# A decode step of adaLN, grouped-query attention and a token MLP: wider matmuls, another order of the rounds, and 96 rows of the output weights in transfers of 8 rows

## The chip, the cores and the metric

The kernel runs on one core of one Trainium2 chip. The metric is the time of one execution in microseconds (us) on the device; the number to compare is the median over several executions. Three executions of the kernel before took 396.08, 396.34 and 397.13 us.

## What is computed

All arithmetic is float32. There are four sequences (B = 4), each with one new token of width D = 512, 32 query heads in 8 groups of 4 (HKV = 8, REP = 4), and caches of 4096 keys and values of width 128 for each group. F = 1792.

```python
mod = silu(c) @ w_mod                 # (4, 512) @ (512, 6*512): sa, ca, ga, sb, cb, gb
h = layernorm(x) * (1 + ca) + sa
q = h @ wq                            # 4 x 32 heads of 128
o = softmax(q @ k^T / sqrt(128)) @ v  # k, v: (4, 8, 4096, 128), 4 queries share one k, v
x = x + ga * (o @ wo)
h = layernorm(x) * (1 + cb) + sb
u = gelu(layernorm(h)[:, :, None] * w1 + b1)   # (4, 512, 1792)
x = x + gb * (u @ w2 + b2)
```

Two caches of 67 MB each are read once; with the weights the kernel reads 157.32 MB.

## The kernel before, in words

One pair of a sequence b and a key head h is called head i, with i = 8 b + h from 0 to 31. For each head one tile of keys (2 MB, `load_k`, L168) and one tile of values (2 MB, `load_v`, L173) are loaded. Those tiles, the query weights and the modulation weights share a ring of five buffers (L35), so a load may be issued once the tile five places before it in the ring has been used. All loads are issued from SP, in the order of the program: keys of head i+3, then values of head i+1. Behind the values of heads 0 to 7 follows 1 MB of output weights each (`wo_t`, L181), which stay; behind heads 2, 4 and 31 follow modulation weights. The keys of head 31 come between the values of heads 28 and 29, and the last loads are the values of head 29 and 30 in two pieces each, those of head 31 in four, and 1 MB of modulation weights.

Every instruction stands where the code puts it: no scheduler moves it, and each engine takes its instructions in program order. A head passes these steps:

- `scores(i)` (L200): eight matmuls, 512 keys each, into four groups of 32 output partitions; then VectorE takes the maximum (L208).
- `colmax(i)` (L211) and `expo(i)` (L219): the maximum is brought together over the partitions by a transpose (L214), a small reduction (L216) and a small matmul (L223), and ScalarE takes the exponential (L228).
- `transposes(i)` (L231): eight transposes of the exponentials, one matmul for the sums (L237), and a copy to SBUF (L238).
- `values(i)` (L248): 32 matmuls with 128 columns, one for every 128 of the 4096 values; then a copy `po` (L259).
- `project_a(i)` (L266) folds the four partition groups and divides by the sum (`pt`, copied to `oT` at L271); `project_b(i)` (L274) multiplies by the output weights in 16 matmuls of 128 columns (L282) and adds into `acc` (L290).

Round i of the main loop (L446) does these for several heads: loads, `transposes(i+1)`, `project_a(i-1)`, `scores(i+2)`, `project_b(i-1)`, `colmax(i+2)`, `expo(i+2)`, a piece of the epilogue of the sequence before, `values(i)`. The epilogue (L362) is the second layer norm and the MLP of a sequence whose eight heads are done: `expand` on VectorE (L354), Gelu on ScalarE (L379), `contract` on TensorE (L359). In the profile its pieces stand in the first five rounds of the next sequence. The last sequence is done in `finish` (L391). In round 25 the gate of the residual is folded into the output weights of head 31 (`fold_gate`, L429), so that its projection can be added to the residual in PSUM (`pgx`).

In the profile a float32 matmul is two weight loads and two multiplications; a transpose is one of each.

Of the kernel before, what the change touches and what calls it, by code (L numbers as in the profile page):

```python
# [23 lines left out]
# 1/sqrt(v): integer seed RS0 - bits(v) / 2, read as a negative float, then a  # L24
# quadratic step y = y (v y^2 - RS1) and a cubic one y = y ((v y^2 - RS2) v y^2 + RS3);
# the seed's scale makes the product of the steps' leading factors one.
# [5 lines left out]
def adaln_decode(ctx: ExitStack, tc: tile.TileContext, small, x, wmod, wq, kT, v, wo, out):  # L32
# [39 lines left out]
    grp = cst.tile([P, 4, 32], F32, name="grp")  # L72
    dv.tensor_copy(grp, g32.unsqueeze(1).to_broadcast([P, 4, 32]))
    grp = grp.rearrange("p c r -> p (c r)")
    sel0 = g32[:, 0:REP]
    diag = ident.rearrange("p (c r) -> p c r", c=4)[:, :, 0:1]
# [5 lines left out]
    for i in range(2):  # L82
        t = cst.tile([P, 8, 4, 32], F32, name=f"pT{i}")
        dv.memset(t, 0.0)
        pTs.append(t)
    wo_t = [cst.tile([P, REP, D], F32, name=f"wo{h}") for h in range(HKV)]
    prep = cst.tile([P, 4, B, P], F32, name="prep")
    osb = cst.tile([P, B, P], F32, name="osb")

# [24 lines left out]
    dv.tensor_mul(sT.rearrange("p k b -> p (k b)"), sg, cT)  # L114

# [36 lines left out]
    px = ps_e.tile([P, B, P], F32, name="px", tag="e")  # L152
    for b in range(B):
        for c in range(4):
            mm(px[32 * c:32 * c + 32, b, :], ident[0:B, b:b + 1].to_broadcast([B, 32]),
               xr[:, c * P:(c + 1) * P], start=True, stop=True)
# [15 lines left out]

    def load_v(i):  # L173
# [6 lines left out]
        if i < HKV:  # L180
            nc.sync.dma_start(wo_t[i], wo[i])  # L181
# [5 lines left out]
    def modmm(pm, t, steps):  # L187
        for b, k in steps:
            for c in range(4):
                mm(pm[32 * c:32 * c + 32, b, :], sT[:, k, b:b + 1].to_broadcast([P, 32]),  # L190
                   WM[t][:, k, c * P:(c + 1) * P], start=(k == 0), stop=(k == 3))

    def mod(t):
        pm = ps_e.tile([P, B, P], F32, name=f"pm{t}", tag="e")
        modmm(pm, t, [divmod(e, 4) for e in range(4 * B)])
        return pm
# [14 lines left out]
    def colmax(i):  # L211
        s, m = S[i]
        pm = ps_m.tile([1, P], F32, name="pm", tag="m")
        nc.tensor.transpose(pm, m, ident)  # L214
        mx = wk.tile([1, 32], F32, name="mx")
        dv.tensor_reduce(mx, pm.rearrange("o (c r) -> o r c", c=4), axis=AX.X, op=OP.max)  # L216
        S[i] = [s, mx]

    def expo(i):  # L219
        s, mx = S[i]  # L220
        pb = ps_m.tile([P, 1], F32, name="pb", tag="m")
        for c in range(4):
            mm(pb[32 * c:32 * c + 32, :], mx, neg1, start=True, stop=True)  # L223
# [7 lines left out]
    def transposes(i):  # L231
        s, p, l = S.pop(i)
        pt = s.rearrange("p (k n) -> p k n", k=8)
        for k in range(8):
# [3 lines left out]
        dv.tensor_copy(pTs[i % 2][:, :, :, 0:REP],  # L238
                       pt.rearrange("p k (c r) -> p k c r", c=4)[:, :, :, 0:REP])
        rl = wk.tile([P, 1], F32, name="rl")  # L240
        dv.reciprocal(rl, pl)
        sel = wk.tile([P, REP], F32, name="sel", bufs=3)
        dv.tensor_scalar(sel, sel0, rl, None, op0=OP.mult)
# [4 lines left out]
    def values(i, ks):  # L248
        if ks[0] == 0:
            PV[i] = ps_v.tile([P, DH], F32, name="pv")  # L250
        pv = PV[i]
        for k in ks:
            for c in range(4):
                mm(pv[32 * c:32 * c + 32, :], pTs[i % 2][:, k, c, :], VT[i][:, k * 4 + c, :],  # L254
                   start=(k == 0), stop=(k == 7))
        if ks[-1] < 7:
            return
        po = wk.tile([P, DH], F32, name="po")
        dv.tensor_copy(po, pv)  # L259
        SP[i] = (SEL.pop(i), po)  # L260

    ACC = {}

    OT = {}

    def project_a(i):  # L266
        sel, po = SP.pop(i)
        pt = ps_m.tile([P, REP], F32, name="pt", tag="m")
        mm(pt, po, sel, start=True, stop=True)  # L269
# [4 lines left out]
    def project_b(i, pa=None):  # L274
        b, h = divmod(i, HKV)
        oT = OT.pop(i)
        folded = pa is not None
        if not folded:
            pa = ps_m.tile([P, P], F32, name="pa", tag="m")
        for g in range(REP):  # L280
            for c in range(4):
                mm(pa[32 * c:32 * c + 32, :], oT[:, g:g + 1].to_broadcast([P, 32]),  # L282
                   wo_t[h][:, g, c * P:(c + 1) * P], start=(g == 0 and not folded), stop=(g == REP - 1))
        if folded:
            return
        if h == 0:
            ACC[b] = wk.tile([P, P], F32, name="acc")
            dv.tensor_copy(ACC[b], pa)
        elif h < HKV - 1:
            dv.tensor_add(ACC[b], ACC[b], pa)  # L290
            if h == HKV - 2:
                ap_ = wk.tile([P, P], F32, name="ap")
                dv.tensor_mul(ap_, ACC.pop(b), prep[:, 1, b])
                dv.tensor_add(ap_, ap_, prep[:, 0, b])
                EP[b] = ap_
        else:
            x1 = XK[:, b]
            dv.tensor_mul(x1, pa, prep[:, 1, b])
            dv.tensor_add(x1, x1, EP.pop(b))

    EP = {}
# [3 lines left out]
    def stats(xin):  # L305
# [3 lines left out]
        dv.tensor_mul(sm_, st.unsqueeze(1).to_broadcast([P, 4, 6]), diag.to_broadcast([P, 4, 6]))  # L309
# [13 lines left out]
    def adaln(b, pst):  # L323
# [4 lines left out]
            a, XK[:, b], mean, prep[:, 3, b], op0=OP.subtract, op1=OP.mult))  # L328
        dv.scalar_tensor_tensor(h1, a, r, prep[:, 2, b], op0=OP.mult, op1=OP.add)
        return h1, stats(h1)  # L330

    def bcast(h1, pb=None):
        if pb is None:
            pb = ps_e.tile([P, 4, P], F32, name="phb", tag="e")
        for c in range(4):
            mm(pb[:, c, :], ident[:, 32 * c:32 * c + 1].to_broadcast([P, P]), h1, start=True, stop=True)
# [24 lines left out]

    def epilogue(b):  # L362
        stm = stats(XK[:, b])
# [4 lines left out]
        hb, wr = affine(pst, bcast(h1))  # L368
# [152 lines left out]
```

## Time and profile before

| | |
|---|---|
| median of three executions | 396.34 us (396.08 to 397.13) |
| profiled execution, from the first to the last instruction | 394.4 us |
| TensorE, matmuls | 288.9 us busy, 5414 records |
| TensorE, weight loads | 194.4 us busy, 5414 records |
| VectorE | 151.4 us busy, 487 instructions |
| ScalarE | 96.4 us busy, 119 instructions |
| mean granted TensorE clock | 0.943 |
| read from memory | 157.32 MB, 399 GB/s over the span |

The profile shows one execution. Its own span is 394.4 us; the median of the timed executions lies 1.9 us above it, which is taken as what lies around the span. A row of a timeline gives the start in us, the length in us, the engine, the line, the operation, and in brackets the idle time before it with what ended that. A count behind a row is that of merged instructions. In the rows by stretches (windows) each engine's busy time is followed by the number of its instructions; the last three numbers are the granted TensorE clock, the busy share of the 16 DMA engines, and GB/s.

### The profile page before, as it was taken

How to read it: one execution, taken by the hardware profiler on the slowest of the kernel's cores; microseconds unless marked ns; L12 is line 12 of the kernel's file. 1: busy time of each engine (PE TensorE's matmuls, PEld its weight loads, DVE VectorE, ACT ScalarE, POOL GpSimd, SP SyncE). 2: the span in 40 equal slices, each digit the busy share in tenths (PEclk: the TensorE clock that was granted, in tenths of full speed). 3: DMA queues.
4: the chain of work that ended last, by engine and by line, in shares of the span. 5: the costliest groups of instructions: out<-in, count | busy, mean ns of one | idle time of the engine just before them, and what ended most of it. 6: DMA issues, size and time to landing. Idle time of an engine off the chain costs nothing.

```text
span 394.4 us, 11762 instructions
## 1 busy us (share of the span) xinstructions
PE 288.9 (73%) x5414; PEld 194.4 (49%) x5414; DVE 151.4 (38%) x487; ACT 96.4 (24%) x119; POOL 0.7 (0%) x6
## 2 busy tenths in 40 slices
PE   0976785539967586778677787779776787897884
PEld 0122444408745444556455455557544464675763
DVE  4222222203222232556432334546323345763266
ACT  1001111101110111136641011348411010685125
POOL 0000000000000000000000000000000000000000
PEclk9989689959999889999999899989999898999999
DMA  8999999999999999999999999999999999999700
GB/s 321 425 430 437 431 419 433 420 430 433 429 420 432 429 429 429 427 432 429 429 421 429 430 434 429 424 425 431 432 429 427 425 429 434 427 425 417 289 8 2
DMA packets 12720, 158.08 MB, mean 401 GB/s; under 512 B 1516, under 2 KB 1532, under 8 KB 1920
## 3 DMA queue, kind: packets, MB, share of 16 engines
q1 hardware_dynamic: 12672, 157.34, 93.9%
q8 instruction: 42, 0.69, 0.6%
q14 instruction: 6, 0.05, 0.0%
HBM read 157.32 MB, written 0.01 MB: 399 GB/s over the span
## 4 chain that ended last, share of the span: by engine, by line
DMA 56%; PE 29%; DVE 8%; ACT 4%; issue 1%; SPq 0%; ACTq 0%; DVEq 0%
DMA k<-in_kT 43%; DMA v<-in_v 11%; PE s L205 10%; PE pv L254 5%; DVE m L208 3%; PE s L126 2%; PE s L235 2%; DMA sm<-in_small 2%; PE py L359 2%; DVE u L354 1%; PE pa L282 1%; ACT uu L414 1%; PE pm L190 1%; ACT p L228 1%; PE qs L141 1%
## 5 line engine op out<-in xcount | busy, mean ns | idle before, releaser
L205 PE MATMUL s<-k,QT 128*32 128x512 f32 x512 | 74.0, 703 | 40.3 <-DMA k<-in_kT 40.2
L228 ACT ACTIVATE p<-s,nm 128x1024 f32<-128x1024 f32 x32 | 35.6, 1114 | 234.5 <-DVE nm L225 234.5
L208 DVE TENSOR_REDUCE m<-s 128x1 f32<-128x1024 f32 x32 | 39.2, 1225 | 101.5 <-PE s L205 101.5
L254 PE MATMUL pv<-v,pT 128*32 128x128 f32 x2048 | 64.5, 277 | 5.6 <-DMA v<-in_v 4.5
L254 PEld LDWEIGHTS pv<-v,pT 128*32 128x32 f32 x2048 | 56.2, 111 | 7.6 <-DMA v<-in_v 5.3
L205 PEld LDWEIGHTS s<-k,QT 128*32 128x32 f32 x512 | 14.7, 119 | 66.4 <-DMA k<-in_kT 41.4
L282 PEld LDWEIGHTS pa<-wo,oT 128*32 128x32 f32 x992 | 30.2, 116 | 22.3 <-issue 21.2
L235 PE MATMUL s<-ident,p 128*128 128x128 f32 x256 | 36.4, 286 | 0.7 <-ACT p L228 0.4
L282 PE MATMUL pa<-wo,oT 128*32 128x128 f32 x992 | 34.6, 282 | 0.8 <-DVE oT L271 0.8
L235 PEld LDWEIGHTS s<-ident,p 128*128 128x128 f32 x256 | 28.6, 145 | 6.9 <-issue 6.3
L259 DVE COPY po<-pv 128x128 f32<-128x128 f32 x32 | 9.3, 290 | 41.9 <-PE pv L254 41.9
L354 DVE TENSOR_SCALAR u<-hb,wr,sm 128x512 f32<-128x512 f32 x42 | 20.0, 542 | 2.5 <-PE py L359 2.2
L214 PE MATMUL pm<-ident,m 128*1 128x128 f32 x32 | 8.7, 271 | 16.7 <-DVE m L208 16.7
L379 ACT ACTIVATE u<-u 128x1024 f32<-128x1024 f32 x21 | 20.9, 1047 | 0.1
L238 DVE COPY pT<-s 128x128 f32<-128x128 f32 x32 | 9.3, 290 | 24.8 <-PE s L235 23.6
L223 PE MATMUL pb<-neg,mx 1*32 1x1 f32 x256 | 7.6, 176 | 13.3 <-DVE mx L216 13.3
L214 PEld LDWEIGHTS pm<-ident,m 128*1 128x1 f32 x32 | 2.5, 79 | 28.8 <-DVE m L208 28.8
L126 PE MATMUL s<-wm,sT 128*4 128x512 f32 x16 | 9.6, 771 | 9.7 <-DVE sT L114 9.7
L269 PE MATMUL pt<-sel,po 128*128 128x4 f32 x64 | 11.8, 254 | 4.5 <-DVE po L259 2.9
L228 ACT ACT_TABLE_LOAD x9 | 11.5, 1283 | 13.2 <-DVE nm L225 13.1
L223 PEld LDWEIGHTS pb<-neg,mx 1*32 1x32 f32 x256 | 4.9, 103 | 19.5 <-DVE mx L216 19.5
L359 PE MATMUL py<-u,sm 128*32 128x128 f32 x336 | 11.6, 276 | 2.9 <-ACT u L379 2.9
(114 smaller groups left out, 233.1 us busy)
## 6 DMA issues: line engine op xcount, KB each, us to landing
k<-in_kT SPq DMA_DIRECT2D x32, 2048.0 KB, 22.6
v<-in_v SPq DMA_DIRECT2D x29, 2048.0 KB, 22.5
wq<-in_wq SPq DMA_DIRECT2D x4, 2048.0 KB, 18.0
wo<-in_wo SPq DMA_DIRECT2D x8, 1024.0 KB, 23.1
v<-in_v SPq DMA_DIRECT2D x5, 1024.0 KB, 19.0
wm<-in_wmod SPq DMA_DIRECT2D x2, 2048.0 KB
wm<-in_wmod SPq DMA_DIRECT2D x2, 1024.0 KB, 16.4
v<-in_v SPq DMA_DIRECT2D x1, 512.0 KB, 20.2
```

The lines of the kernel that those rows point to most:

```text
L126: mm(s0[0:B, t * D:(t + 1) * D], sT[:, k, :], wm01[:, t, k, :], start=(k == 0), stop=(k == 3))
L205: mm(s[32 * c:32 * c + 32, n * 512:(n + 1) * 512], QT[:, b, h, :], KT[i][:, (n * 4 + c) * 512:(n * 4 + c + 1) * 512], start=True, stop=True)
L208: dv.tensor_reduce(m, s, axis=AX.X, op=OP.max)
L223: mm(pb[32 * c:32 * c + 32, :], mx, neg1, start=True, stop=True)
L228: nc.scalar.activation(p, s, AF.Exp, bias=nm, accum_out=l)
L235: nc.tensor.transpose(pt[:, k, :], p[:, k * P:(k + 1) * P], ident)
L254: mm(pv[32 * c:32 * c + 32, :], pTs[i % 2][:, k, c, :], VT[i][:, k * 4 + c, :], start=(k == 0), stop=(k == 7))
L269: mm(pt, po, sel, start=True, stop=True)
L282: mm(pa[32 * c:32 * c + 32, :], oT[:, g:g + 1].to_broadcast([P, 32]), wo_t[h][:, g, c * P:(c + 1) * P], start=(g == 0 and not folded), sto ...
L354: dv.tensor_scalar(u[:, e, :], hb, wr[:, j:j + 1], b1[:, j:j + 1], op0=OP.mult, op1=OP.add)
L359: mm(py[32 * c:32 * c + 32, :], w2[:, j:j + 1].to_broadcast([P, 32]), u[:, e, c * P:(c + 1) * P], start=(j == 0), stop=(j == NF - 1))
L379: nc.scalar.activation(u, u, AF.Gelu_apprx_tanh)
```

## The change

The change has these parts.

1. **Wider matmuls.** `values` takes two tiles of 128 values in one matmul of 256 columns (16 for a head in place of 32) and leaves two halves, which `project_a` adds with two matmuls in place of one. `project_b` of sequences 0 to 2 uses 512 columns (4 matmuls in place of 16), one for each of the four queries in a partition group of its own; the groups are added once for a sequence (`fold_groups`, 4 matmuls). For sequences 0 and 1 `contract` does the same (14 matmuls and a fold in place of 56). The modulation is computed for the four sequences at once, eight partitions for each in every group of 32 (`sT8`, 16 matmuls in place of 64). In `expo` one matmul takes the place of four, and the reduction ahead of it writes its result four times (L228 after). All in all there are 1740 matmuls and transposes in place of 2857.
2. **Rounds that begin with scores.** `scores(i+2)` now stands ahead of `project_a` and `transposes`; `values(i)` stands in two halves around the small matmul of `expo`. The pieces of the epilogue are spread over seven rounds.
3. **The end.** The keys of head 31 are issued one place earlier, in front of the values of head 28. The last rounds are written out: `scores(31)` now stands in front of `values(28)`. The gate is folded into the weights of heads 30 and 31, and head 30's projection goes to `pgx` as well. The modulation matmuls of `finish` stand together; three small stores take the place of one.
4. **Output weights.** For heads 0, 1 and 2 the first 32 of 128 rows (8 KB each) are loaded in four transfers of 8 rows, and the other 96 rows in one.

The core of the diff:

```diff
+    def load_wo(h):
+        first = 32 if h < 3 else 0
+        for e in range(0, first, 8):
+            nc.sync.dma_start(wo_t[h][e:e + 8], wo[h, e:e + 8])
+        nc.sync.dma_start(wo_t[h][first:], wo[h, first:])
...
         if i < HKV:
-            nc.sync.dma_start(wo_t[i], wo[i])
+            load_wo(i)
...
-        mx = wk.tile([1, 32], F32, name="mx")
-        dv.tensor_reduce(mx, pm.rearrange("o (c r) -> o r c", c=4), axis=AX.X, op=OP.max)
+        mx = wk.tile([1, 4, 32], F32, name="mx")
+        dv.tensor_reduce(mx, pm.rearrange("o (c r) -> o r c", c=4).unsqueeze(1).to_broadcast([1, 4, 32, 4]),
+                         axis=AX.X, op=OP.max)
...
         for k in ks:
-            for c in range(4):
-                mm(pv[32 * c:32 * c + 32, :], pTs[i % 2][:, k, c, :], VT[i][:, k * 4 + c, :],
-                   start=(k == 0), stop=(k == 7))
+            q = k % 4
+            mm(pv[32 * q:32 * q + 32, :], pTs[i % 3][:, k, :],
+               VT[i][:, k * 2:(k + 1) * 2, :].rearrange("p j d -> p (j d)"), start=(k < 4), stop=(k >= 12))
...
+        if b < B - 1:
+            pa = ps_m.tile([P, D], F32, name="pa", tag="m")
+            for g in range(REP):
+                mm(pa[32 * g:32 * g + 32, :], oT[:, g:g + 1].to_broadcast([P, 32]), wo_t[h][:, g, :],
+                   start=True, stop=True)
...
+    def fold_groups(pool, acc, tag):
+        pc = pool.tile([P, P], F32, name="pc", tag=tag)
+        for c in range(4):
+            mm(pc[32 * c:32 * c + 32, :], first, acc[:, c * P:(c + 1) * P], start=True, stop=True)
+        return pc
...
+        load_k(i + 3)
+        if i == NS - 5:
+            load_k(NS - 1)
         load_v(i + 1)
+        scores(i + 2)
+        if i:
+            project_a(i - 1)
         transposes(i + 1)
...
+    scores(n + 3)
+    transposes(n + 2)
+    colmax(n + 3)
+    expo(n + 3)
+    values(n, range(16))
+    fold_gate(gate, (6, 7))
+    next(epi)
...
+    project_a(n + 3)
+    project_b(n + 3, x3)
+    next(epi)
+    finish(B - 1, pgx[:, 0], x3, epi)
```

How instructions move is seen in three places. First TensorE before, from the scores of head 30 to the projection behind the scores of head 31; `k_3587`, `k_3721`, `v_3589` and `v_3723` are the keys of heads 30 and 31 and the values of heads 28 and 29 before:

```order
L205 MATMUL s_3745<-k_3587,QT 32x512 x8
L282 MATMUL pa<-wo_122,oT 32x128 x16
L214 MATMUL pm<-ident,m 1x128
L223 MATMUL pb<-neg_102,mx 32x1 x4
L359 MATMUL py<-u,sm 32x128 x16
L254 MATMUL pv<-v_3589,pT_115 32x128 x32
L359 MATMUL py<-u,sm 32x128 x8
L235 MATMUL s_3745<-ident,p 128x128 x8
L237 MATMUL pl<-l,grp 128x1
L269 MATMUL pt<-sel,po 128x4
L205 MATMUL s_3877<-k_3721,QT 32x512 x8
L282 MATMUL pa<-wo_123,oT 32x128 x16
```

The same engine after, from the transposes of head 29 to the values of head 28; here the keys of head 31 are `k_2611` and the values of head 28 `v_2613`:

```order
L247 MATMUL s_2615<-ident,p 128x128 x8
L249 MATMUL pl<-l,grp 128x1
L315 MATMUL pq<-wo_126,oT 32x128 x16
L226 MATMUL pm<-ident,m 1x128
L394 MATMUL py<-u,sm 32x128 x16
L235 MATMUL pb<-neg_102,mx 128x1
L217 MATMUL s_2798<-k_2611,QT 32x512 x8
L247 MATMUL s_2722<-ident,p 128x128 x8
L249 MATMUL pl<-l,grp 128x1
L226 MATMUL pm<-ident,m 1x128
L235 MATMUL pb<-neg_102,mx 128x1
L269 MATMUL pv<-v_2613,pT_117 32x256 x16
```

The scores of head 31 moved ahead of the values of head 28, with their own transposes of head 30 and reductions between; the projection of head 27 (`pq`) stands ahead of the reduction of head 30 (`pm`), and no contraction stands behind the values any more. Second, VectorE after from the copy of head 28's values to the copy of head 29's:

```order
L273 COPY po<-pv 128x256
L498 TENSOR_TENSOR wo_130<-wo_130,gate 128x512 x2
L389 TENSOR_SCALAR u<-hb,wr,sm 128x512 x4
L251 COPY pTl<-s_2798 128x32x4
L256 RECIPROCAL rl<-pl 128x1
L258 TENSOR_SCALAR sel<-g_107,rl 128x8
L299 COPY oT<-pt 128x4
L324 TENSOR_TENSOR acc<-acc,pq 128x128
L273 COPY po<-pv 128x256
```

And before, at the same place:

```order
L259 COPY po<-pv 128x128
L238 COPY pT_115<-s_3745 128x32x4
L241 RECIPROCAL rl<-pl 128x1
L243 TENSOR_SCALAR sel<-g_107,rl 128x4
L271 COPY oT<-pt 128x4
```

Two multiplications by the gate and four expansions of the epilogue now stand between the copy `po` and the copy `oT` that the projection of head 28 waits for. Third, TensorE after, from the values of head 31 (`v_2928`) to the statistics of the last layer norm:

```order
L282 MATMUL pvl<-v_2928,pTl 32x128 x32
L576 MATMUL pgx<-ep,ident 128x128
L297 MATMUL pt<-sel,po 128x4
L315 MATMUL pgx<-wo_130,oT 32x128 x16
L394 MATMUL py<-u,sm 32x128 x24
L348 MATMUL pst<-epsr,ones 128x24
L349 MATMUL pst<-stm,ones 128x24
```

And before, with the same values as `v_3955`:

```order
L254 MATMUL pv<-v_3955,pT_117 32x128 x24
L484 MATMUL pgx<-ap,ident 128x128
L254 MATMUL pv<-v_3955,pT_117 32x128 x8
L359 MATMUL py<-u,sm 32x128 x8
L269 MATMUL pt<-sel,po 128x4
L282 MATMUL pgx<-wo_126,oT 32x128 x16
L314 MATMUL pst<-epsr,ones 128x24
L315 MATMUL pst<-stm,ones 128x24
```

Of the contraction of sequence 2, 24 matmuls now stand between the last projection and the matmul that adds up its statistics (`pst` from `stm`), where 8 stood ahead of the projection.

More of the change, by code (lines that the diff above doesn't have):

```diff
@@ L393, in finish @@
         U = [uu[j // 8][:, j % 8] for j in range(NF)]
[L394 removed]
+        stm = stats(xp, b)
         dv.tensor_copy(XK[:, b], xp)
[L396 removed]
         pst = gather(stm)
[L398 removed]
+        modmm(pg, 5)
         h1, stm = adaln(b, pst)
@@ L476, in adaln_decode @@
                 dv.tensor_copy(dst, pm)
[L477 to L485 removed]
+        if i == NS - HKV - 2:
+            gate = spread_gate()
+        if i == NS - HKV or i == NS - HKV + 1:
+            e = 3 * (i - NS + HKV)
+            fold_gate(gate, range(e, e + 3))
+    n = NS - 4
+    load_v(n + 1)
+    scores(n + 2)
+    project_a(n - 1)
+    transposes(n + 1)
+    project_b(n - 1)
+    colmax(n + 2)
+    next(epi)
+    expo(n + 2)
+    scores(n + 3)
[5 more added lines that the diff above has]
+    next(epi)
+    load_v(n + 2)
+    transposes(n + 3)
+    project_a(n)
+    project_b(n)
+    values(n + 1, range(16))
+    next(epi)
+    load_v(n + 3)
+    values(n + 2, range(8))
+    project_a(n + 1)
+    project_b(n + 1)
+    ep = cst.tile([P, P], F32, name="ep")
+    residual(ep, ACC.pop(B - 1))
+    values(n + 2, range(8, 16))
+    pgx = ps_s.tile([P, 8, P], F32, name="pgx", tag="s")
+    x3 = pgx[:, 4]
+    project_a(n + 2)
+    project_b(n + 2, x3)
+    for ks in ((0, 1, 2, 3), (4, 5), (6,), (7,)):
+        values_last(n + 3, ks)
+    mm(x3, ident, ep, start=False, stop=False)
+    project_a(n + 3)
+    project_b(n + 3, x3)
     next(epi)
[L487 to L489 removed]
+    finish(B - 1, pgx[:, 0], x3, epi)
 def kernel(**inputs):
```

246 lines of the change are left out of this document (130 added, 116 removed).

## Prediction

> **What bounds the kernel now.** I read the page first: its slices and the queues of its DMA part.
>
> ```profile
> span 394.4 us, 11762 instructions
> PE 288.9 (73%) x5414; PEld 194.4 (49%) x5414; DVE 151.4 (38%) x487; ACT 96.4 (24%) x119; POOL 0.7 (0%) x6
> DMA  8999999999999999999999999999999999999700
> GB/s 321 425 430 437 431 419 433 420 430 433 429 420 432 429 429 429 427 432 429 429 421 429 430 434 429 424 425 431 432 429 427 425 429 434 427 425 417 289 8 2
> q8 instruction: 42, 0.69, 0.6%
> ```
>
> From the second slice to the 37th the 16 DMA engines are busy and move about 429 GB/s, or 26.8 GB/s each; the rest is the end behind the loads. The q8 row is a second stream on the same engines: 42 packets of 0.69 MB in all, 16 KB each. Shared out over TensorE's 10828 weight loads and multiplications it is 64 bytes for each, so I read it as the fetching of TensorE's program. Next the stretches (windows) at the end of the loads; the last two numbers are the DMA share and GB/s.
>
> ```profile
> 366.00:368.00 2.00, 1.49 (x36) 1.40 (x38) 0.66 (x4) 0.27 (x1) 0.00 (x0) 1.00 0.99 416
> 368.00:369.00 1.00, 1.00 (x47) 1.00 (x40) 0.29 (x1) 0.00 (x0) 0.00 (x0) 1.00 0.71 297
> 372.00:373.00 1.00, 1.00 (x44) 1.00 (x37) 0.64 (x3) 0.00 (x0) 0.00 (x0) 1.00 0.55 209
> 374.00:375.00 1.00, 1.00 (x26) 0.88 (x29) 0.00 (x0) 0.00 (x0) 0.00 (x0) 1.00 0.47 188
> 375.00:376.00 1.00, 0.85 (x22) 0.52 (x11) 0.40 (x2) 0.00 (x0) 0.00 (x0) 1.00 0.02 8
> ```
>
> The share does not fall from 0.99 to 0 at once: near 368.3 us half of the engines have nothing left, and the other half work on until 375.2. So one half is 6.9 us late. A tile is there only when its last row is, so the late half sets every landing. If the fetches all fall on eight engines, each has 42/8 = 5.25, and 6.9/5.25 = 1.3 us for one is plausible, since 16 KB at 26.8 GB/s take 0.61 us without the switching. That the fetches are the cause is my inference.
>
> Then the chain of waits, and when the keys of head 30 land: they were issued at 325.04 and took 23.6 us, so 348.6.
>
> ```profile
> 305.64 23.52 DMA k<-in_kT
> 329.21 3.54 PE s L205 x16
> 340.80 1.90 PE s L205 x16
> 349.44 1.90 PE s L205 x16
> 359.42 1.90 PE s L205 x16
> 372.23 1.08 PE pv L254 x37
> 377.83 0.42 PE pst L315 x2
> ```
> ```profile
> 325.04 0.33 SPq L171 DMA_DIRECT2D k<-in_kT  x1
> k<-in_kT SPq DMA_DIRECT2D x1, 2048.0 KB, 23.6
> ```
>
> The last DMA of the chain ends at 329.2. From there to the end it is computing, round behind round, since TensorE has fallen behind the loads. What counts is therefore two things: when the keys land, and how long the chain is from there. From the keys of head 30 (348.6) to the sum of the last statistics (377.83) it is 29.2 us, and 16.6 more to 394.4.
>
> **Part 1, the loads.** The program loses 1117 matmuls of 2857, each two loads and two multiplications: 10828 records less 4468 are 6360, a factor of 0.59, so about 25 fetches in place of 42. The late half's 6.9 us become 4.1: 2.8 us earlier. The 96 rows of 8 KB: a head's 128 rows are eight for each engine; after, 96 rows are six for each, and if the 32 others go to eight engines only, those have ten. Over three heads this moves six rows, 48 KB, which at 26.8 GB/s are 1.8 us. No row tells on which engines they fall: on the early half the late half ends 1.8 us earlier, on the late half 1.8 later, spread evenly nothing changes. I take the early half; the range holds the even spread, and the late half is a rival. Then the early half ends at 370.1 and the late at 370.6, so the landings are 4.6 us earlier, and the keys of head 30 land at 344.0. [...]
>
> The 14 additional transfers each occupy SP's queue for 0.3 to 0.5 us; the loads behind them are issued some 20 us ahead of their landing, which covers it. Without that cover it would be 2 us for each head.
>
> **Part 2, the wide matmuls.** Their price is in these rows of the timeline, which also carry the sum of part 3.
>
> ```profile
> 349.20 0.29 DVE L238 COPY pT<-s 128x128 f32<-128x128 f32 x1 [0.77 <-PE s L235]
> 349.37 1.92 PE L205 MATMUL s<-k,QT 128*32 128x512 f32 x16
> 349.74 0.16 DVE L271 COPY oT<-pt 128x4 f32<-128x4 f32 x1
> 351.36 1.22 DVE L208 TENSOR_REDUCE m<-s 128x1 f32<-128x1024 f32 x1 [1.46 <-PE s L205]
> 352.64 0.27 PE L214 MATMUL pm<-ident,m 128*1 128x128 f32 x1 [0.47 <-DVE m L208]
> 352.95 0.28 DVE L216 TENSOR_REDUCE mx<-pm 1x32 f32<-1x128 f32 x1 [0.17 <-PE pm L214]
> 353.29 0.24 PE L223 MATMUL pb<-neg,mx 1*32 1x1 f32 x8 [0.37 <-DVE mx L216]
> 353.67 1.91 DVE L354 TENSOR_SCALAR u<-hb,wr,sm 128x512 f32<-128x512 f32 x4
> 354.35 1.93 PE L254 MATMUL pv<-v,pT 128*32 128x128 f32 x64
> 356.35 0.29 DVE L259 COPY po<-pv 128x128 f32<-128x128 f32 x1 [0.77 <-PE pv L254]
> 344.81 1.52 PE L359 MATMUL py<-u,sm 128*32 128x128 f32 x48
> 326.11 2.48 DVE L435 TENSOR_TENSOR wo<-wo,pgb 128x512 f32<-128x512 f32 x4 [0.27 <-PE pgb L432]
> ```
>
> Sixteen records of 512 columns (scores) take 1.92 us, 64 of 128 columns (values) 1.93: both are 8192 columns. So width itself saves no time on the array; 32 records of 256 columns are again 8192, about 1.9 us. Only the modulation truly shrinks, and it is off the chain. What the width brings is the shorter program of part 1.
>
> **Part 3, the chain from the keys of head 30.** The gain of the early keys of head 31 is that two heads' scores are done before the values of head 28 land. I add up the written-out order with the rows above and these:
>
> ```profile
> 370.16 0.29 DVE L259 COPY po<-pv 128x128 f32<-128x128 f32 x1 [1.46 <-PE pv L254]
> 370.50 0.39 PE L269 MATMUL pt<-sel,po 128*128 128x4 f32 x2 [0.41 <-DVE po L259]
> 371.14 1.08 PE L282 MATMUL pa<-wo,oT 128*32 128x128 f32 x32 [0.25 <-DVE oT L271]
> 372.04 2.02 PE L254 MATMUL pv<-v,pT 128*32 128x128 f32 x48
> 375.12 0.29 DVE L259 COPY po<-pv 128x128 f32<-128x128 f32 x1 [1.89 <-PE pv L254]
> 376.11 1.08 PE L282 MATMUL pgx<-wo,oT 128*32 128x128 f32 x32 [0.25 <-DVE oT L271]
> ```
>
> - Keys of head 30 to scores of head 31: scores 2.0 (349.37 to 351.36), reduction 1.2; behind it on VectorE now stands the copy `oT` (0.15), and the projection of head 27 (0.9 until TensorE is free, 371.14 to 372.04) stands ahead of `pm`; `pm` to `pb` 0.65 (352.64 to 353.29), and 0.4 for the reduction of four times as many elements (0.28 us for 128 elements here, 0.62 for 512 at L435). 5.4 us with the hand-overs.
> - Scores of head 31 to values of head 28: the same without the projection, 4.4.
> - Values of head 28 to the projection of head 28: 2.0; copy of 256 columns 0.4; gate twice 0.62; four expansions 1.9; `pTl` to `oT` 0.7 (349.20 to 349.90). They overlap by 0.3: 6.0. TensorE waits 2.5 us in this, which it did not before.
> - To the values of head 31: projection 0.9, values of 29 2.0, copy 0.4, half of 30's values 0.9, fold and copy 0.65, projection 0.9, the other half 1.1, copy 0.4, fold 0.65, projection 0.9; 9.3 with hand-overs.
> - Values of head 31: 2.0. The last piece of them lands 24.3 us behind the keys of head 30 (five tiles of 2 MB at 429 GB/s), the chain is there at 26.6, so TensorE stays behind.
> - To the statistics' sum: copy to projection 1.0 (375.12 to 376.11), projection 0.9, then 24 matmuls of contraction, 48 records, 1.3, and 0.2: 3.4. Before it was 2.7 (375.12 to 377.83).
>
> Together 30.5 against 29.2: 1.3 longer, because the waiting epilogue work and the gate were moved into this stretch. Behind it nothing changes but stores (three issues in place of one, ready before the last one) and modulation matmuls, which stand beside VectorE and ScalarE: 16.6 us.
>
> **TensorE's clock** is the term that I can only bound:
>
> ```profile
> 325.60:329.00 3.40, 1.73 (x17) 1.67 (x15) 3.09 (x9) 0.00 (x0) 0.00 (x0) 1.00 0.97 410
> 308.50:311.90 3.40, 3.40 (x19) 0.83 (x23) 0.00 (x0) 0.00 (x0) 0.00 (x0) 0.50 0.97 414
> core 0: 394.4 us, clock 0.943
> ```
>
> The first two rows are stretches, the third the mean of the whole run. After 1.7 us of waiting the clock of the next stretch was 0.50, and the scores at 329.21 took 3.54 in place of 1.90. The new wait of 2.5 us can bring such a stretch of 3.4 us, in which TensorE loses at most half, 1.7; nothing, if it falls on waiting. I take 0.8, near the middle.
>
> **Sum.** -4.6 + 1.3 + 0.8 = -2.5 us: the profiled span of 394.4 becomes 391.9. The median of the runs lies 1.9 us above that span, which I carry over: 393.8. 0.3% is 1.2 us, about what a measurement here can tell from no change.
>
> **Rivals.**
>
> A. The loads set the end after all: if the steps on VectorE overlap more than I allow, the chain is no longer than before and the clock stays, so only the landings count: 396.3 - 4.6 = 391.7. For it speaks that TensorE has 3 us of waits in my chain to give back; against, that the gate and the expansions stand ahead of `oT` in program order. 0.15.
>
> B. Slower: the small transfers crowd. A packet of 8 KB takes 0.31 us at an engine's pace, twelve of them 3.7. All eight rows of a transfer go to eight neighbouring partitions; if four engines had to share one way into the memory, a packet takes 1.2, and twelve cost 11.0 us more. The early half then ends at 381.1, 5.9 later than the late half now, and with the longer chain the time is 396.3 + 5.9 + 2.1 = 404. It decides from 4.6 us on all twelve, 0.4 for each packet. No transfer in the trace goes to so few partitions under load, so no row speaks against it; the gain in part 1 would not exist. 0.12. [...]
>
> C. The rows fall on the late half: the landings are 2.8 - 1.8 = 1.0 earlier, and 396.3 - 1.0 + 2.1 = 397.4; evenly spread 395.6. Nothing in the views decides. 0.05 and 0.03.
>
> D. The chain is longer still: the clock drops fully (1.7) and the waits on VectorE add 0.6: 395.3, not to be told from no change. For it the 0.50 rows; against, that such stretches are few (a mean clock of 0.943). 0.13.
>
> **How the numbers follow.** Forecast 0.52, A 0.15, D 0.13, B 0.12, C 0.08. Faster: forecast and A, 0.67. Same: D and the even spread, 0.16. Slower: B and the late half, 0.17. The range leaves out B and the late half (0.17): from A's 391.7 with 0.3 below, to D's 395.3 and the even spread's 395.6 with 0.8 above: 391.4 to 396.4.
>
> **What would show it.** Right: about 25 packets in the q8 row; the DMA share falling from 0.99 to 0 within a microsecond or so near 370.5; the keys of head 30 landing near 344; the chain of waits without a DMA from about there; a TensorE wait for `oT` of about 2.5 us behind the values of head 28; the sum of the last statistics near 375.3. Wrong: two steps in the DMA share that remain 3 us or more apart (C), loads that end behind 375 (B), or a last chain that waits for the values of head 31 (A).

## The result and the profile after

The changed kernel took 415.76 us (median of four executions, 414.84 to 418.21), the kernel before beside it 396.21 us (395.99 to 397.13). The ratio is 1.050 (95% interval 1.047 to 1.053): slower by 19.6 us, where 2.5 us less were forecast. Ratios here leave out executions that lie more than 1.5% above the fastest of the same kernel; only one kernel below (32 and 96 rows) had such, two of its four.

The page of the changed kernel: span, engines, throughput in 40 slices of 10.3 us, program fetches.

```profile
span 413.8 us, 7345 instructions
PE 309.4 (75%) x3180; PEld 154.0 (37%) x3180; DVE 180.6 (44%) x494; ACT 99.2 (24%) x121; POOL 0.7 (0%) x6
GB/s 328 431 423 423 324 379 276 337 302 428 421 426 426 428 424 432 427 426 428 422 428 427 426 431 428 426 428 425 428 426 424 426 428 428 425 417 407 113 2 2
q8 instruction: 25, 0.41, 0.4%
```

The fetches are 25, as forecast. But slices 5 to 9 sum to 1618 GB/s in place of 5 x 429: 527/429 of a slice of 10.35 us, 12.7 us of loading are lost between 41 and 93 us, where the output weights of heads 0 to 2 arrive. The stretches there, first of the kernel after, then two of the kernel before (the last two numbers are DMA share and GB/s):

```profile
46.00:51.00 5.00, 4.74 (x31) 2.35 (x29) 1.69 (x4) 0.56 (x2) 0.00 (x0) 0.71 1.06 246
56.00:61.00 5.00, 1.41 (x8) 0.46 (x12) 0.00 (x0) 0.00 (x0) 0.00 (x0) 0.50 1.04 442
81.00:86.00 5.00, 5.00 (x27) 3.08 (x30) 2.06 (x6) 0.00 (x0) 0.00 (x0) 0.50 0.98 205
```
```profile
46.00:51.00 5.00, 4.70 (x26) 2.69 (x26) 1.03 (x6) 0.24 (x2) 0.00 (x0) 0.50 1.04 442
81.00:86.00 5.00, 0.69 (x4) 0.20 (x8) 0.00 (x0) 0.00 (x0) 0.00 (x0) 0.50 0.99 426
```

The DMA engines are just as busy (a share of 0.98 where it was 0.99, from 81 to 86 us) with half the bytes (205 GB/s where they were 426), so a packet takes twice as long: those of 8 KB that start in that stretch take 621 ns in the mean, where 309 ns are usual in the kernel before. Starved of transfers, the engines would show a lower share, as at the end of the loads before (0.47 at 188 GB/s from 374 to 375 us). The end of the chain of waits after:

```profile
340.29 22.83 DMA k<-in_kT
363.16 1.92 PE s L217 x16
369.20 1.85 PE s L217 x16
373.90 1.86 PE pv L269 x32
379.94 1.91 PE pq L315 x32
381.85 2.62 PE pv L269 x32
391.26 1.75 PE pvl L282 x64
...
396.78 0.35 PE pst L349 x2
```

The keys of head 30 land at 340.29 + 22.83 = 363.12, 14.5 us later than before (348.6) and 19.1 later than forecast. Behind them the chain goes nearly as forecast in its parts, with one large exception, the projection of head 28 and the values of head 29 (1.91 and 2.62 us). The timeline shows why; the bracket is the idle time before an instruction and what ended it.

```profile
375.83 0.42 DVE L273 COPY po<-pv 128x256 f32<-128x256 f32 x1 [1.74 <-PE pv L269]
376.17 1.28 DVE L498 TENSOR_TENSOR wo<-wo,gate 128x512 f32<-128x512 f32 x2
377.37 1.91 DVE L389 TENSOR_SCALAR u<-hb,wr,sm 128x512 f32<-128x512 f32 x4
379.73 0.15 DVE L299 COPY oT<-pt 128x4 f32<-128x4 f32 x1
379.94 1.91 PE L315 MATMUL pq<-wo,oT 128*32 128x128 f32 x32 [2.58 <-DVE oT L299]
```
```profile
380.02:383.43 3.41, 3.41 (x52) 2.57 (x56) 0.29 (x1) 0.41 (x1) 0.00 (x0) 0.50 0.95 382
```

TensorE waits 2.58 us for `oT`, behind two gate products and four expansions on VectorE. The last row above is a stretch: the granted clock behind that wait is 0.50 for 3.41 us. In the 3.41 us ahead of it, from 376.61 to 380.02, the clock was 1.00 and TensorE was busy for 0.83 us; so the low clock came behind a stretch that was not all idle, with the wait of 2.58 us in it.

### The profile page after: what moved, and what is told of

Same layout as the page of the kernel before. It is cut to its first block, busy times and chain, and to the rows that moved or that the text cites. A ratio compares the mean times of both kernels' runs of the same rounds, so it can differ in the third digit from the quotient of the medians.

```text
span 413.8 us, 7345 instructions
## 1 busy us (share of the span) xinstructions
PE 309.4 (75%) x3180; PEld 154.0 (37%) x3180; DVE 180.6 (44%) x494; ACT 99.2 (24%) x121; POOL 0.7 (0%) x6
## 4 chain that ended last, share of the span: by engine, by line
DMA 68%; PE 23%; DVE 5%; ACT 2%; issue 1%; SPq 0%; ACTq 0%
DMA k<-in_kT 40%; DMA v<-in_v 21%; PE s L217 5%; DMA wo<-in_wo 5%; PE pv L269 5%; PE s L131 2%; PE s L247 2%; DMA sm<-in_small 2%; PE pa L308 2%; PE pt L297 1%; ACT uu L472 1%; PE pq L315 1%; PE pb L235 1%; DVE u L389 1%; DVE acc L324 1%; DVE mx L228 1%
## 5 line engine op out<-in xcount | busy, mean ns | idle before, releaser
L269 PE MATMUL pv<-v,pT 128*32 128x256 f32 x992 | 67.2, 390 | 3.6 <-DMA v<-in_v 2.7
L269 PEld LDWEIGHTS pv<-v,pT 128*32 128x32 f32 x992 | 27.8, 111 | 19.9 <-PE pm L226 4.9
L297 PEld LDWEIGHTS pt<-sel,po 128*128 128x128 f32 x126 | 18.6, 212 | 32.9 <-issue 25.1
L308 PE MATMUL pa<-wo,oT 128*32 128x512 f32 x192 | 29.6, 694 | 1.0 <-DVE oT L299 1.0
L273 DVE COPY po<-pv 128x256 f32<-128x256 f32 x31 | 13.2, 424 | 28.5 <-PE pv L269 28.5
L228 DVE TENSOR_REDUCE mx<-pm 1x128 f32<-1x512 f32 x32 | 21.5, 672 | 0.7 <-PE pm L226 0.7
L297 PE MATMUL pt<-sel,po 128*128 128x4 f32 x126 | 21.4, 275 | 0.5 <-DVE po L273 0.5
L324 DVE TENSOR_TENSOR acc<-acc,pa 128x512 f32<-128x512 f32 x21 | 14.4, 687 | 14.3 <-PE pa L308 14.3
L235 PEld LDWEIGHTS pb<-neg,mx 1*128 1x128 f32 x64 | 9.3, 182 | 17.7 <-DVE mx L228 17.3
L235 PE MATMUL pb<-neg,mx 1*128 1x1 f32 x64 | 12.1, 256 | 4.4 <-DVE mx L228 4.2
```

The costliest lines, as they stand in the source:

```text
L228: dv.tensor_reduce(mx, pm.rearrange("o (c r) -> o r c", c=4).unsqueeze(1).to_broadcast([1, 4, 32, 4]), axis=AX.X, op=OP.max)
L235: mm(pb, mx.rearrange("o c r -> o (c r)"), neg1, start=True, stop=True)
L269: mm(pv[32 * q:32 * q + 32, :], pTs[i % 3][:, k, :], VT[i][:, k * 2:(k + 1) * 2, :].rearrange("p j d -> p (j d)"), start=(k < 4), stop=(k ...
L297: mm(pt, po[:, c * DH:(c + 1) * DH], sel[:, c * REP:(c + 1) * REP], start=(c == 0), stop=(c == n - 1))
L308: mm(pa[32 * g:32 * g + 32, :], oT[:, g:g + 1].to_broadcast([P, 32]), wo_t[h][:, g, :], start=True, stop=True)
```

## The experiments: the output weights

Theories: **(N)** eight neighbouring rows crowd on one way into the memory, the prediction's rival B; **(O)** every transfer in which the engines carry other rows than in a whole transfer of 128 disturbs, the one of 96 rows too; **(I)** 14 more transfers delay SP's queue; **(R)** the rest of the change. First the changed kernel with whole transfers.

```diff
-        first = 32 if h < 3 else 0
+        first = 0
```

> The changed kernel with each head's output weights loaded in one transfer of 128 rows, as before; wide matmuls and order stay. Crowding on the way into the memory (by neighbouring rows or by rows off their usual engines): the stretch from 41 to 91 us goes back to about 430 GB/s, the landings return to those of before or up to 2.8 us earlier (25 fetches of TensorE's program in place of 42), the chain behind the keys of head 30 stays about 4.9 us longer as in the changed kernel: 398 to 401 us. Late issue on SP's queue: the same time, since the 14 additional transfers are gone too. If the order or the wide matmuls themselves cost the time: 410 us or more.

Measured: 402.06 us, ratio 1.0146 (1.0122 to 1.0171). That is 1.1 us more than the upper end of what I expected, and still 13.7 us of the 19.6 hang on how three megabytes are loaded. The page's throughput has no gap left:

```profile
GB/s 319 429 429 431 423 420 433 422 419 435 423 426 423 426 429 428 424 431 424 426 427 424 428 428 426 431 420 424 431 428 431 424 428 423 427 416 404 76 2 2
```

The other way round, the kernel before with the split alone (the same five transfers in place of `wo_t[i] <- wo[i]`, for i below 3):

> The kernel before, with only the output weights of heads 0 to 2 loaded in 4 transfers of eight rows and one of 96. Crowding, by whichever of the two: the landings come 12 to 14.5 us later, 408 to 411 us. If the loss needs the new order or the wide matmuls: 396 to 398 us.

Measured: 410.8 us, ratio 1.0385 (1.0364 to 1.0406), 14.8 us longer. The loss needs neither the wide matmuls nor the order. Which part of the split? First the eight rows apart from each other, then no transfer of eight rows:

```diff
-        for e in range(0, first, 8):
-            nc.sync.dma_start(wo_t[h][e:e + 8], wo[h, e:e + 8])
+        for e in range(first // 8):
+            nc.sync.dma_start(wo_t[h][e:first:4], wo[h, e:first:4])
...
-        for e in range(0, first, 8):
-            nc.sync.dma_start(wo_t[h][e:e + 8], wo[h, e:e + 8])
+        for e in range(0, first, 32):
+            nc.sync.dma_start(wo_t[h][e:e + 32], wo[h, e:e + 32])
```

> The changed kernel, but each transfer of eight rows takes every fourth of the first 32 rows instead of eight neighbours: as many transfers, bytes and rows, but the eight partitions lie apart. Crowding of neighbouring partitions: most of the loss goes, within 2 us of the kernel with whole transfers. Rows off their usual engines, the 96-row transfer above all: more than half of the loss stays, 407 to 414 us. Late issue on SP's queue: 415.8 us as before it.

> The changed kernel with the first 32 rows of heads 0 to 2 in one transfer, then the 96 others: no transfer of eight rows is left, the 96-row transfer stays. Crowding by the small transfers alone: within 2 us of the kernel with whole transfers. If the 96-row transfer (six rows for each engine, not eight) is what disturbs: 406 us or more, and the throughput from 49 to 54 us is still low. Late issue: like whole transfers.

Measured: 412.61 us, ratio 1.0426 (1.0404 to 1.0448), and ratio 1.0338 (1.0320 to 1.0356), about 409.4 us. The second rests on two executions, 408.57 and 410.18 us; the two others took 415.17 and 416.52 at the same granted clock (0.887 to 0.891 in all four), and the median of all four is 412.67. Only 3.2 us go with the neighbours; without any transfer of eight rows at least 7.3 us above whole transfers remain. N alone is refuted. Now the kernel before, with other pieces of the same bytes: two transfers of 64 rows, or four of all 128 rows and 2 KB each.

```diff
-            nc.sync.dma_start(wo_t[i], wo[i])
+            for e in range(0, P, 64 if i < 3 else P):
+                n = 64 if i < 3 else P
+                nc.sync.dma_start(wo_t[i][e:e + n], wo[i, e:e + n])
...
-            nc.sync.dma_start(wo_t[i], wo[i])
+            for g in range(REP if i < 3 else 1):
+                n = 1 if i < 3 else REP
+                nc.sync.dma_start(wo_t[i][:, g:g + n], wo[i][:, g:g + n])
```

> The kernel before, with the output weights of heads 0 to 2 in two transfers of 64 rows each, and nothing of eight rows. If engines that leave the rows they have in a whole transfer meet others on the same way into the memory, two engines would share each way: a head takes 4.9 us in place of 2.4, 7 us in all, about 403 us. If only transfers of eight rows, or rows that don't divide evenly (six for each engine), disturb: 396 to 397 us.

> The kernel before, with the output weights of heads 0 to 2 in four transfers of 128 rows, 2 KB of each row: as many additional transfers for SP's queue, but every engine keeps its rows. Crowding: 396 to 397 us. If the number of transfers, their issue or their completions cost the time: 404 us or more.

Measured: 410.54 us, ratio 1.0362 (1.0339 to 1.0385), and 397.45 us, ratio 1.0030 (1.0015 to 1.0046). Two stretches of the kernel with 64 and 64 rows, and the same stretches of the one that divides columns:

```profile
61.00:66.00 5.00, 5.00 (x49) 2.02 (x41) 1.23 (x1) 0.00 (x0) 0.00 (x0) 0.50 1.05 264
66.00:71.00 5.00, 2.07 (x45) 1.72 (x45) 0.68 (x3) 1.21 (x2) 0.00 (x0) 0.84 1.00 254
```
```profile
61.00:66.00 5.00, 3.49 (x72) 3.13 (x72) 0.42 (x2) 1.20 (x2) 0.00 (x0) 0.68 1.09 448
66.00:71.00 5.00, 2.53 (x24) 1.55 (x20) 0.95 (x5) 0.00 (x0) 0.00 (x0) 0.84 1.00 429
```

Nine more transfers cost 1.4 us when every row takes part; three more cost 14.5 when the rows are divided. I is out. O fits, but it is not shown: in the trace before, packets that follow one another come in eights on the engines, with rows of 16, 8, 4 and 2 KB alike, but no view tells which engine carries which row, and each of these kernels divides the rows of the source along with those of the tile, so that reading and writing are not told apart. The 7 us that I had expected, an estimate with two engines on each way that no run shows, were half of what was measured. The two stretches say where the rest is: in 10 us at about 259 GB/s 2.6 MB went by, and the weights of a head are 1 MB. So the tiles beside them are slowed too, and their packets in the traces show it: between 38 and 95 us, 239 of 866 packets of 16 KB (an output weight's row has 8) take 650 ns or more with 64 and 64 rows, 4 of 1105 in the kernel before, 5 of 1073 with divided columns. Why it spreads so far no run shows.

Last, the eight-row transfers by themselves: twelve added to the whole transfers of the kernel before, as neighbours, then every fourth row.

```diff
+            for e in range(0, 32 if i < 3 else 0, 8):
+                nc.sync.dma_start(wo_t[i + 4][e:e + 8], wo[i, e:e + 8])
             nc.sync.dma_start(wo_t[i], wo[i])
...
+            for e in range(4 if i < 3 else 0):
+                nc.sync.dma_start(wo_t[i + 4][e:32:4], wo[i, e:32:4])
             nc.sync.dma_start(wo_t[i], wo[i])
```

> The kernel before with all its whole transfers, and the twelve transfers of eight neighbouring rows added, into the places of output weights that are loaded later: 0.79 MB more. If the eight neighbours crowd as the prediction's rival put it: 11 us and more, 407 us. If the rows of the 96-row transfer, off their usual engines, are the larger part: the difference between neighbours and every fourth row (3 us) and the added bytes (1.8 us over all engines, at most 3.7 us on eight), 397 to 403 us.

> The kernel before with the twelve additional transfers of eight rows (beside its whole transfers), now of every fourth of the first 32 rows instead of eight neighbours (those gave 404.8 us). If neighbours are what disturbs in transfers of eight rows: only the bytes are left, 0.79 MB, 397.9 us if they spread in time over all engines, at most 399.7 us if eight engines carry them. If eight rows in themselves disturb: 404 us or more.

Measured: 404.78 us, ratio 1.0224 (1.0194 to 1.0253), and 399.1 us, ratio 1.0072 (1.0053 to 1.0091). Every fourth row costs 3.1 us, between the two prices for its bytes (estimates at 429 GB/s: 0.79 MB over all engines 1.8, over eight 3.7), and neighbours 5.7 us more, 0.47 us each (404.78 us lies between the two times that I expected, 407 for rival B and 397 to 403 for O). So a transfer of eight rows is not dear in itself. In the changed kernel the neighbours made 3.2 us, so this price depends on what stands beside. The stretch from 46 to 51 us, of neighbours and of every fourth row:

```profile
46.00:51.00 5.00, 5.00 (x29) 3.67 (x31) 1.19 (x6) 0.66 (x2) 0.00 (x0) 0.50 1.02 279
```
```profile
46.00:51.00 5.00, 5.00 (x31) 3.33 (x29) 1.19 (x6) 0.23 (x2) 0.00 (x0) 0.54 1.01 426
```

## The experiments: the order

With whole transfers 6 us remained. The next kernel keeps the wide matmuls and takes the rounds and the last heads in the order of the kernel before; part of its edit:

```diff
-    for i in range(NS - 4):
+    for i in range(NS - 1):
...
+        transposes(i + 1)
+        if i:
+            project_a(i - 1)
         scores(i + 2)
-        if i:
-            project_a(i - 1)
-        transposes(i + 1)
...
-        if i == NS - HKV or i == NS - HKV + 1:
+        if i in (NS - HKV, NS - HKV + 1, NS - HKV + 2):
```

> The wide matmuls with whole transfers of the output weights, but the rounds in the order of the kernel before (values last, the keys of head 31 in their old place, and the end as it was, with the gate's products and the expansions in earlier rounds). If the order of the end, with its new wait of TensorE and the clock behind it, makes the 6 us: 395 to 397 us. If the wide matmuls themselves or the lower clock over the whole run make it: 400 us or more.

Measured: 397.43 us, ratio 1.0035 (1.0021 to 1.0048). The order costs 4.6 us. Is it the wait? Gate and expansions were moved out of it:

```diff
     values(n, range(16))
-    fold_gate(gate, (6, 7))
-    next(epi)
     load_v(n + 2)
...
     project_b(n)
+    next(epi)
     values(n + 1, range(16))
```

> The changed kernel with whole transfers of the output weights (402.1 us), and with the last two gate products in the round of head 26 and four expansions behind the projection of head 28, so that nothing stands on VectorE between the values of head 28 and the copy for their projection. If the new wait of TensorE and the half clock behind it are what the order costs: the projection of head 28 follows 2.5 us earlier, the values of head 29 take 1.9 in place of 2.9, 397 to 399 us. If the order costs because the values of four heads now stand behind the last scores: 401 us or more.

Measured: 397.8 us, ratio 1.0059 (1.0035 to 1.0084). Its timeline at the same place:

```profile
362.60 0.42 DVE L273 COPY po<-pv 128x256 f32<-128x256 f32 x1 [1.73 <-PE pv L269]
364.20 0.15 DVE L299 COPY oT<-pt 128x4 f32<-128x4 f32 x1
364.41 1.08 PE L315 MATMUL pq<-wo,oT 128*32 128x128 f32 x32 [0.29 <-DVE oT L299]
365.31 1.91 PE L269 MATMUL pv<-v,pT 128*32 128x256 f32 x32
```

From the start of `po` to the projection are 1.8 us in place of 4.1 (375.83 to 379.94 in the changed kernel); projection and values take 1.08 and 1.91 in place of 1.91 and 2.62. That is 2.3 + 0.8 + 0.7 = 3.8 of the 4.3 us; in the kernel with whole transfers the two take 1.64 and 2.89, which gives 3.8 as well. What then is left of the order is 0.4 us above the old one, within the intervals of the two: neither gain nor loss. The place of head 31's keys, undone alone:

```diff
-        if i == NS - 5:
-            load_k(NS - 1)
...
     n = NS - 4
+    load_k(NS - 1)
     load_v(n + 1)
```

> The changed kernel with whole transfers, and with the keys of head 31 loaded behind the values of head 28, as in the kernel before. If the early keys are a gain: the scores of head 31 wait for the landing near 358.4 in place of starting at 356.8, 1.6 us longer, 403 to 404 us. If the early keys are what costs the time, 398 us or less; if they do nothing, 402 us.

Measured: 406.32 us, ratio 1.0271 (1.0239 to 1.0302), 4.3 us longer than with early keys by the medians, not 1.6. The chain of waits at the scores of head 31, and two stretches around their start:

```profile
337.41 20.94 DMA k<-in_kT
358.39 3.10 PE s L217 x16
361.49 1.50 PE s L247 x8
```
```profile
354.70:358.30 3.60, 0.00 (x0) 0.00 (x0) 0.14 (x1) 1.21 (x2) 0.00 (x0) 1.00 0.98 410
358.99:362.40 3.41, 3.41 (x21) 1.20 (x10) 0.86 (x1) 0.00 (x0) 0.00 (x0) 0.50 1.01 420
```

The scores start at 358.39, as expected, but TensorE has nothing at all to do in the 3.6 us ahead of it, the clock behind is 0.50, and they take 3.10 in place of 1.9 us. This does not explain the 4.3 us: the low clock has passed when the projection of head 28 comes (1.08 us long, from 370.77), the values of head 29 end 1.5 us later than with early keys (373.62 and 372.17), and the two profiled executions, 405.04 and 403.29 us, differ by 1.75. The other executions lie further apart (405.25 to 408.42 against 400.16 to 403.55), and why is open. In this order the early keys are needed; the order itself just doesn't pay.

## The experiments: the place of the tiles

One thing did not fit. With 25 fetches in place of 42 the landings should have come 2.8 us earlier; in the kernel with whole transfers the keys of head 30 land at 348.6 (issued at 329.55, 19.1 us), exactly as before. The stretches at the end of the loads, wide matmuls in the old order:

```profile
368.00:369.00 1.00, 1.00 (x47) 1.00 (x40) 0.27 (x1) 0.20 (x1) 0.00 (x0) 1.00 1.05 422
370.00:371.00 1.00, 0.95 (x20) 0.29 (x12) 0.00 (x0) 0.00 (x0) 0.00 (x0) 1.00 0.89 350
371.00:372.00 1.00, 0.51 (x4) 0.51 (x4) 0.92 (x3) 0.00 (x0) 0.00 (x0) 1.00 0.58 231
375.00:377.00 2.00, 1.75 (x40) 1.36 (x36) 0.45 (x2) 0.00 (x0) 0.00 (x0) 1.00 0.01 4
```

The halves end near 370.8 and 375, so their distance shrank from 6.9 to about 4.2 us, as forecast for 25 fetches; but it is the early half that ends later. In the trace, packets of 16 KB take 611 ns in the kernel before and 611 to 624 (mean 616) in the wide kernels so far. In the built programs the new constants had moved the ring of tiles from byte 113408 of each partition, a multiple of 256, to 110464, which is not. 128 bytes put that right, and do wrong to the kernel before:

```diff
+    pad = cst.tile([P, 32], F32, name="pad")
```

> The wide matmuls in the order of before (397.4 us), with 128 bytes of padding in front of the ring of key and value tiles, so that these begin at a multiple of 256 bytes in each row as they do in the kernel before. If the place of the tiles makes the packets of 16 KB take 611 to 624 ns where they took 611: all packets back at 611, the loads' end up to 2 us earlier, 395 to 396.5 us. If the wide matmuls do it in another way: no change, 397.4 us.

> The kernel before with 128 bytes of padding in front of the ring of key and value tiles, which moves them off the multiple of 256 bytes. If the place makes the packets slower: packets of 611 to 624 ns, the loads' end about 1 to 2 us later, 397 to 398 us. If not: 396.0 us and all packets at 611.

Measured: 395.03 us, ratio 0.9967 (0.9954 to 0.9980), and 398.71 us, ratio 1.0070 (1.0051 to 1.0090). The end of the loads with padding in the wide kernel, then in the kernel before:

```profile
368.00:369.00 1.00, 0.45 (x9) 0.11 (x2) 0.59 (x2) 0.00 (x0) 0.00 (x0) 1.00 0.67 270
371.00:372.00 1.00, 1.00 (x48) 1.00 (x41) 0.00 (x0) 0.00 (x0) 0.00 (x0) 1.00 0.41 172
372.00:373.00 1.00, 1.00 (x27) 0.61 (x15) 0.29 (x1) 0.00 (x0) 0.00 (x0) 1.00 0.10 41
```
```profile
370.00:371.00 1.00, 1.00 (x44) 1.00 (x40) 0.29 (x1) 0.00 (x0) 0.00 (x0) 1.00 0.77 317
375.00:377.00 2.00, 1.95 (x42) 1.16 (x38) 0.54 (x2) 0.00 (x0) 0.00 (x0) 1.00 0.53 215
377.00:379.00 2.00, 1.75 (x54) 1.41 (x50) 0.45 (x2) 0.00 (x0) 0.00 (x0) 1.00 0.28 111
```

In the first the halves end near 368 and 372.2, the late one 3.0 us earlier than before (375.2). In the second near 370.5 and 378, 2.2 and 2.8 us later than before. The packets change sides too: 611 ns with the wide matmuls, 611 to 624 in the kernel before. The queue rows show the sum, without and with padding in the wide kernel: 94.2% of 395.1 us is 372.2, 94.3% of 392.4 is 370.0.

```profile
q1 hardware_dynamic: 12680, 157.34, 94.2%
```
```profile
q1 hardware_dynamic: 12680, 157.34, 94.3%
```

What moved is the place written to; why that makes the packets slower no run shows. The changed order without its wait, with the same padding:

> The changed order without its new wait (397.8 us), whole transfers, and the 128 bytes of padding that bring the tiles back to a multiple of 256 bytes. If the early scores gain something once the keys land some 2.5 us earlier: 394.5 us or less, below the old order with padding (395.0 us). If the chain behind the scores is the same length either way: 395 to 396 us.

Measured: 395.08 us (394.67 to 399.14), ratio 1.0002 (0.9976 to 1.0028). The median is that of the old order with padding (395.03), but five of twelve executions took 396.49 us or more. It settles that the order gains nothing, not whether it loses a little.

## The experiments: the last stage

In the wide kernels the last expansion ran at half clock (0.50 from 379.78 to 386.60 us, with padding), in the kernel before it did not (1.00 from 382.0 to 390.0). There 64 modulation matmuls stood in that stage, now 16. 48 were put back, their results unused, so this kernel only tests the clock:

```diff
         modmm(pg, 5)
+        modmm(fill[:, 0], 5)
...
+        modmm(fill[:, 1], 5)
         hb, wr = affine(pst, pb)
...
+            if j == 0:
+                modmm(fill[:, 2], 5)
```

> The wide matmuls in the old order with padding (395.0 us), and with 48 further modulation multiplications in the last stage, whose results nothing uses: as many as the kernel before had there. If the half clock of TensorE in the last expansion comes from the idle time that their removal left: a granted clock of 1.00 there and 0.5 to 1 us less, 394 to 394.6 us. If it has another cause: 395 us or more.

Measured: 394.15 us (394.10 to 395.82), ratio 0.9957 (0.9940 to 0.9974), the fastest here. The granted clock from 379.8 us, without and with the filling:

```profile
379.78:386.60 6.82, 4.85 (x77) 2.78 (x80) 6.45 (x18) 6.67 (x8) 0.00 (x0) 0.50 0.00 0
```
```profile
376.39:379.80 3.41, 3.41 (x65) 3.03 (x57) 2.29 (x11) 0.00 (x0) 0.00 (x0) 0.50 0.02 5
379.80:386.60 6.80, 5.46 (x124) 4.23 (x124) 5.66 (x19) 5.09 (x7) 0.00 (x0) 1.00 0.01 2
```

The clock in the expansion is back at 1.00. That the 0.9 us come from it is not shown. The profiles are of the slowest of the six executions with the filling (395.82) and of the fastest of the eight without (394.13), and from the broadcast ahead of the expansion to the end both take 13.5 us (380.46 to 394.0, and 378.87 to 392.4). With the filling a low stretch stands ahead of the expansion instead, and in it 64 records of modulation matmuls, half of them filling, take 3.48 us on the chain. Whether the five faster executions have such a stretch is open.

## Why the prediction was wrong

Taken apart, the 19.6 us are: split of the output weights 13.7 us (415.76 to 402.06), order 4.6 (to 397.43), place of the tiles 2.4 (to 395.03), and what is left of the wide matmuls -1.0 (396.0 before), 19.7 in all. Each figure is the difference of two neighbouring kernels, so their sum has to come out; the split (14.8) and the place of the tiles (2.7) were also measured on the kernel before.

- **The step that failed** is the one on the output weights in part 1: "96 rows are six for each, and if the 32 others go to eight engines only, those have ten" and "I take the early half", -1.8 us. It counted bytes for each engine and took every byte at 26.8 GB/s, whatever row it goes to, and nothing in the trace spoke for the early half. Runs of eight packets in the trace before and of six in the one after agree with the eight and six rows; that the 32 others go to eight engines, on which the 1.8 us rest, no run shows. The runs put +13.7 us (on the kernel before +14.8) in its place: transfers that take a part of the rows bring the throughput down to about half (205 GB/s in place of 426 from 81 to 86 us) and slow other tiles' packets. That an engine then carries other rows than in a whole transfer is the reading that fits, not one that is shown.
- **Rival B** had the side right. That four engines share one way into the memory, from which its 11 us are worked out, no run shows; its eight neighbouring rows cost 5.7 us for twelve added transfers beside whole ones, and in the changed kernel 3.2 of the 13.7; it overlooked the larger transfers beside them, which cost more. So its side came out partly by luck. Its sign did come: the loads end behind 375 us, with a DMA share of 0.77 from 384 to 385 and 0.04 from 389 to 390. Its 0.12 was too little for a pattern that no row of the trace showed.
- **The fetches**: "2.8 us earlier", and 25 in number. Right: 3.0 us, in the kernel with padding, where the keys of head 30 also land 2.8 us earlier (345.9). That fetches make one half of the engines late, an inference then, is supported by the distance of 4.2 us where 4.1 were forecast. In the changed kernel the gain was hidden, besides the split, by a part of the change that part 1 did not see: new constants moved the tiles, 2.4 us.
- **Width saves no array time**: right, 32 records of 256 columns take 1.86 us where 64 of 128 took 1.93.
- **The chain**: forecast 30.5 us from the keys of head 30 to the sum of the statistics and 0.8 for the clock; measured 363.12 to 396.78, 33.7. The first three steps (5.4, 4.4, 6.0) took 6.1, 4.7 and 6.0, the last two together (5.4) 5.5; the first leaves out a contraction of 1.01 us (L394), which stands between `pm` and `pb`. The wait for `oT` came with 2.58 us for 2.5. The fourth, 9.3, took 11.3: the half clock cost 1.5 there, near its bound of 1.7, not the 0.8 set aside for it.
- **"Behind it nothing changes"**: 17.0 us for 16.6. The clock is 0.50 from 400.5 to 407.3 us, and the broadcast ahead of the expansion (L371) takes 1.52 us in place of 0.99 (L336 before). That the modulation matmuls had kept the clock up before is likely: with 48 of them put back it was 1.00 in the expansion.

Landings 19.1 us late against the forecast, chain 2.4, end 0.4: together 21.9, the difference between the spans of 391.9 and 413.8.

## What to carry to other kernels

A load that is divided by rows is not the same load. All four divisions by rows here cost 7 us or more and the one by columns 1.4, so divide by columns, and look at GB/s against DMA share, which shows a slow packet where the share alone shows nothing (205 and 426 GB/s here, at 0.98 and 0.99). After adding constants, look where the big tiles begin. Work that is moved off the chain still stands in a queue: ask what waits behind it on that engine, and what the clock does after the wait (0.50 for 3.41 us behind 2.58 us of waiting here).

## What the runs showed of the hardware

- Divided into 64 and 64 rows, 3 MB of weights cost 14.5 us, and other tiles' packets beside them were slowed (239 of 866 took 650 ns or more, 4 of 1105 in the kernel before); divided by columns 1.4 us.
- Beside whole transfers, eight rows as neighbours cost 0.47 us a transfer more than every fourth row (404.78 and 399.1 us with twelve).
- Tiles that begin 128 bytes off a multiple of 256 lengthened a kernel that loads 157 MB by 2.4 to 2.7 us (397.43 against 395.03, 398.71 against 396.05).
- One half of the DMA engines ended 6.9 us late with 42 fetches and 4.2 us with 25, with the tiles at a multiple of 256.
